# A linear-attention and gated-MLP kernel: the first batch's state add moves into a TensorE product, weight bits go through ScalarE, and the issue table is new

## The chip, the cores and the metric

The kernel runs on one core of one Trainium2 chip. The metric is device time in microseconds, from launch to end, of that one core. Three runs of the kernel before gave 377.19, 381.42 and 382.31 us.

## The reference

Four batches of 768 time steps pass through an attention with a decaying state (8 heads of 48 channels), and its output `x` (768 x 384 for each batch) through a gated layer whose gate mixes the time steps:

```python
for t in range(S):                                   # S = 768
    cur = einsum('bhd,bhe->bhde', u[None] * kt, vt)
    y[:, :, t] = einsum('bhd,bhde->bhe', rt, state + cur)
    state = wt[:, :, :, None] * state + einsum('bhd,bhe->bhde', kt, vt)
...
h = maximum(x @ w_in, 0.0)
u, v = h[..., :512], h[..., 512:]
v_n = (v - mean(v)) / sqrt(var(v) + 1e-06)
gated = u * (einsum('ts,bsd->btd', w_spatial, v_n) + b_spatial[None, :, None])
return gated @ w_out
```

Inputs and output are float32, except `w_in` and `w_out`, which are float64.

## The kernel before, in words

**Tiling.** A batch is cut into 6 chunks of 128 steps, a chunk into two halves of 64 (`x` = 0 and 1). Chunks are numbered 0 to 23 over all batches; the first batch is chunks 0 to 5. The heads are packed in pairs on 112 partitions (`R`), four pairs side by side (`G`).

**Attention of a chunk.** SyncE loads the decays `W`, the keys `kk`, the queries `rr` and the values `v` (`slot_load`). VectorE builds running products of the decays with two scans (L432 into `F`, L442 in place), then `kk*F` (L445) and `rr*W` (L447); either product may stand on GpSimd. TensorE transposes `kk*F` (L504, tile `pt`; below "the key transposes") and ScalarE copies that to `KT`; TensorE forms the state's increment `pd` for both halves (L562, 48x48 products into the PSUM tile `pp`). `slot_s` then updates the state of each half in two steps: S0 = `pd` + old state (L577 or L579, VectorE) and new state = S0 times the decay at the half's end (L582, VectorE or GpSimd). Three state tiles `SA` go round. TensorE also forms the scores (L487), which VectorE writes into `As` under a mask (L490), and sums the output in the PSUM tile `pyw` from `As` and `v` and from `rr` and the state (L516). In chunks 0 to 5 the bonus term comes from four small TensorE products (L417, tile `pg`, from `rk` = `kk`*`rr`, L412). ScalarE splits the result into a high and a low part for exact products (L600, L607), in chunks 0 to 7 with a TensorE product that subtracts the high part (L604).

**The gated layer.** Each product is three passes, high x high, high x low, low x high (`mm3`, L614 to L616): `ph` for a chunk (3 groups of three products, 512 columns), `pu`, `pv` and `po` for half batches (384 columns).

**The weights.** `split64` (L328 to L357) turns each float64 piece into a high and a low float32r part. A piece is two words per number, `dl` and `dh`; L348 scales `dh` (ScalarE or VectorE), L350 shifts that left by 3 (VectorE), L351 takes the top three bits of `dl` in (VectorE), L352 the sign. There are 10 pieces, 6 of 512 columns and 4 of 384.

**What sets the order.** All operations are collected first. The table `PLAN` names an engine and a start time for each, `plan` sorts by the start times, and the engines get their instructions in that order. Nothing on the chip waits for a time of the table: each engine takes its instructions in turn and waits only for what an instruction reads or overwrites. `fill` puts filler products (`warm`, L854, 128 x 128 of zeros into a corner of `pyw`) on TensorE where the table has a gap on it, until `last`, which stands behind chunk 5.

Of the kernel before, what the change touches and what calls it, by code (L numbers as in the profile page):

```python
# [10 lines left out]
I32 = mybir.dt.int32  # L11
AF = mybir.ActivationFunctionType
# [17 lines left out]
T19r Sdc S9l S4k6 S39x S73 Akk Vmy Vo7 Vu9 A17i G1pt Sc3 Auf Vw8 Vxh V16p A27a G29r Spa A1ek V1hp V1ka V1nn  # L30
A1po G1ut S3c S4l S5u S8c Vfg Tuv Vbj Vf0 Vh4 Vhs Aog Ghl Vl9 Axn Anx Ayb Tla Amp Tol Vq6 Grk Txe Tyf V14x
T17c T18p A1ao T1cf A1di S1f0 A1we V1zy V22k V265 A3bk G3ep Smg A162 V18e V1de V1g1 A1o0 V3lp S1xh A29v V2tt
V2v2 V2zd A36l V3p2 S3vw A4s6 V4x8 S2ic A2tg V4da S1yq A2cw G3y8 S1zz A2e2 V3u9 S450 A58r V5ch S2y9 A3fr
G40w S6e4 A6qj G7n2 S57l A5hr G5rf S6xs A7fr G7ke S218 A2gj G2lj S4vq A5bb V5gc S7wr A85w G87j S1b9 A3d0
V4el V4fo V4hb A4m1 V4o8 S2fu A2x9 V312 V324 V3jg A44m G47p S4ix A4tb V4v8 V4yj V506 A566 V57p S3l3 V3x9
V4im V4jo V4mo A532 V561 T1vz T2fn T2oz A2ro A2uw A2ye Sau Sfu Sel Skj Vz5 T11h Vr3 Vvx Vx5 V11r A159 G11a
G19k A1g0 A1a5 A1go V10u G14q T14z A18y T1at V1ch V1f3 T1gn T1ng V1pk T1s0 T1ux A1xt T1za A20e T21v T2i5
T2k2 A2q1 A2ul A2v9 Snp S10d S1a0 S1ci V1im T1kx V19b V1pc V1rd V1sm A1w3 V1lz V20v A1nq A1sb A21z V1ro G1t8
T1p5 A1r4 T1tm V1vr G1y8 T242 T253 V29i T2by T2db A2f7 T2hl A2io T2qx T2vi T2xg A332 A381 A38p A3b1 V3ch
V3c7 V3ct G3di G3ea G3i4 G3iw A3pt A3t5 V3vk A3nu A417 V45k A3lv A46t V4bm S1dr S1pe S1w8 S1tw V24h T26s  # L40
V1wr V248 V2bb V2ck A2g9 V27u G2g6 A29l A21g A2jq V2bm G2d6 T2aa A2bp T2ec V2fx V2k4 T2m9 T2na V2pf T2t4
T2uh A320 T33h A34z T385 T3e0 T3fx A3uk A40x A42m S22v S271 S2el S2h3 G2o7 T30s V2gz V2l2 V2lm V2ma A2pr
V2s5 V2wr A34p A362 G35i V2r7 V2yf T2ze A30t T34a V35v G389 T3ae T3bf V3ei T3i5 T3jh A3kt T3na A3rt T3y4
T401 T44n A4ai A4eq A4fe S2x0 S2p9 S2vr S2zi V33l T35w V36t V3aa V3d1 V3gb A3sv V3aj V3ne V3dd A3gw V3ro
V3dl V3ks T3d4 A3ej T3kj V3qs V3tc T3vd T3wf V3ye T428 T43l A45r T47g A49g T4ax T4cu T4er A4hd A4je A4k1
A4o9 V4nz V4pk G4q9 G4ss G4tk G4uc V4uz A547 A57b V594 A513 A59w V5ds V4vy A4xj V5as T572 S38o A3i0 S3mc
A3yb S419 A4c5 S4f3 A4p1 T3lu T3qr T3tn A3xa T4zs T519 T58s T5el T5hi T5iy V5ll G5or A5rn V613 T3nv T3pa
T3s7 A3w7 T5t4 T5ul T60w T64c T65t T679 V6h1 G6is A6ro V71b T480 T49h T4gp A4yz T52p T57c T5a8 T5g2 T5ro
T62c V6ja V6nq A6pd V72m T4sf T4tw T4vc A501 T545 T55l T5bp T5d5 T5ke T5lv V5nu G5u3 A5yo V6w6 T736 T74m
T763 T7bn A7dn S7f1 T71q T7a7 T7op T7q5 V7s7 S8hd T7d4 T7ek T7g0 T7hg V7pn Sac2 T4i5 T4jl T4l2 A4n6 T8jj  # L50
T8l0 T8mg T8ul T9fc T9lp V9oc G9q4 A9w2 V9xm T6dn T6f3 T6gk A6ij T7rm T7t2 T7ui T7zr T817 T8b2 V8g6 V8ht
A8jq G8qv T5nb T5os T5q8 A5t2 T7vy T7yb T86p T885 T89m T8ci V8nm V94w A9if V9n1 T4o2 T4pj T4qz A4ug T8pc
T8qt T8s9 T8w2 T91j T930 V975 G9e2 A9ux Va3r Taqj Tarz Tb0e Tb1v Ab3u Sbmd Taie Taju Tam6 Tanm Aau3 Sbjv
# [12 lines left out]
Vahy Aaqc Aaso Gaul Ab4w Ab7x Vbr7 Aalq Ab1u Gb3q S86q A8g2 S8j0 A8wp S90u A9dq S9go A9s2 T9az T9cf T9dv
# [48 lines left out]

GAP, FILL_TO = 0.8, 5

EARLY = 8

NA = 3  # L120

# [870 lines left out]
```

## Time and profile before

| what | value |
|---|---|
| three runs, median (lowest, highest) | 381.42 us (377.19, 382.31) |
| the profiled execution, its own time | 379.98 us |
| its span from the first to the last instruction | 378.2 us |
| mean granted TensorE clock | 0.963 |
| TensorE busy | 361.2 us, 95% of the span |
| VectorE, ScalarE, GpSimd busy | 253.4, 190.4, 107.0 us |

The span is 1.8 us shorter than the profiled execution's time. A granted clock of 1.00 is 2.4 GHz, 0.50 is 1.2 GHz; a stretch between holds some of both. TensorE's ends are modelled, so its busy share says that something was in its pipeline and not that the array was full. "Idle before" an instruction is time in which its engine had nothing running, and the name behind the arrow is what ended it.

### The profile page before, as it was taken

Reading aid. Unit: us, or ns where it says so; the run is one execution under the profiler, and the core shown is the slowest. Engines: PE = TensorE matmul, PEld = TensorE weight load, DVE = VectorE, ACT = ScalarE, POOL = GpSimd, SP = SyncE. Lnnn points to the kernel's source line nnn. Section 1 sums busy time; section 2 is a strip of 40 time slices with the busy share of each in tenths; the row PEclk is TensorE's granted clock in tenths of the full one; section 3 lists DMA queues with packets and bytes.
Section 4 is the critical chain, followed back from the end, with each engine's and each line's share of the span. In section 5 each row is a group of like instructions: output and inputs, shape, how many; then the busy total and the mean of one; then the engine's idle time right before and its main releaser. Section 6 shows DMA issues by size and latency. Waiting matters only on the chain.

```text
span 378.2 us, 13807 instructions
## 1 busy us (share of the span) xinstructions
PE 361.2 (95%) x5994; PEld 327.0 (86%) x5994; DVE 253.4 (67%) x491; ACT 190.4 (50%) x525; POOL 107.0 (28%) x140
## 2 busy tenths in 40 slices
PE   5799899999999999999999999999999999999995
PEld 5777678899889788999988898989989888999995
DVE  6989489999877786867577587656556754342131
ACT  2556578994456437872244138651154336722122
POOL 3505417114314242170401312144620041003111
PEclk9856599999999999999999999999999999999999
DMA  7967447673564645424233637243234420120221
GB/s 207 248 174 221 127 121 234 177 207 105 159 177 118 185 143 167 148 72 156 68 114 92 196 103 223 58 157 85 50 109 146 132 63 5 27 77 2 55 93 66
DMA packets 33023, 47.91 MB, mean 127 GB/s; under 512 B 3264, under 2 KB 21824, under 8 KB 32960
## 3 DMA queue, kind: packets, MB, share of 16 engines
q1 hardware_dynamic: 32960, 47.00, 43.0%
q8 instruction: 48, 0.79, 0.9%
q14 instruction: 15, 0.12, 0.1%
HBM read 42.27 MB, written 4.72 MB: 124 GB/s over the span
## 4 chain that ended last, share of the span: by engine, by line
PE 78%; DMA 8%; DVE 5%; ACT 4%; issue 2%; POOL 2%; SPq 1%; DVEq 0%; POOLq 0%; ACTq 0%
PE pyw L516 9%; PE pv L614 8%; PE pv L615 8%; PE pv L616 8%; PE ph L614 5%; PE ph L616 4%; PE ph L615 4%; PE pu L614 4%; PE po L614 4%; PE po L616 4%; PE po L615 4%; PE pu L615 3%; PE pu L616 3%; DMA kk<-in_tr_dram 3%; PE pp L487 3%; DMA rr<-in_tr_dram 3%
## 5 line engine op out<-in xcount | busy, mean ns | idle before, releaser
L614 PE MATMUL pv<-ws,vh 128*128 128x384 f32 x192 | 66.8, 348 | 0.0
L615 PE MATMUL pv<-ws,vh 128*128 128x384 f32 x192 | 64.9, 338 | 0.6 <-POOL ws L325 0.6
L616 PE MATMUL pv<-ws,vl 128*128 128x384 f32 x192 | 64.8, 338 | 0.0
L720 DVE TENSOR_TENSOR t<-pv,b_sb 128x384 f32<-128x384 f32 x32 | 17.7, 553 | 30.9 <-PE pv L616 30.8
L614 PEld LDWEIGHTS pv<-ws,vh 128*128 128x128 f32 x192 | 36.0, 188 | 1.3 <-ACT ws L323 0.3
L615 PEld LDWEIGHTS pv<-ws,vh 128*128 128x128 f32 x192 | 36.1, 188 | 0.9 <-POOL ws L325 0.9
L616 PEld LDWEIGHTS pv<-ws,vl 128*128 128x128 f32 x192 | 36.1, 188 | 0.0
L724 ACT CAST gh<-t 128x384 fp32r<-128x384 f32 x32 | 15.9, 512 | 38.3 <-POOL t L722 25.6
L614 PE MATMUL pu<-xT,wi 128*128 128x384 f32 x96 | 34.0, 355 | 0.0
L614 PE MATMUL po<-wo,gh 128*128 128x384 f32 x96 | 32.8, 342 | 0.0
L615 PE MATMUL pu<-xT,wi 128*128 128x384 f32 x96 | 32.4, 338 | 0.0
L432 DVE TENSOR_TENSOR_SCAN F<-W,zz 112x512 f32<-112x512 f32 x24 | 29.1, 1212 | 5.0 <-ACT zz L444 3.7
L616 PE MATMUL pu<-xT,wi 128*128 128x384 f32 x96 | 32.4, 337 | 0.0
L615 PE MATMUL po<-wo,gh 128*128 128x384 f32 x96 | 32.3, 336 | 0.0
L616 PE MATMUL po<-wo,gl 128*128 128x384 f32 x96 | 32.3, 336 | 0.0
L614 PE MATMUL ph<-wi,xT 128*128 128x512 f32 x72 | 31.5, 438 | 0.0
L582 POOL TENSOR_TENSOR SA<-S,prod 112x256 f32<-112x256 f32 x22 | 17.5, 797 | 43.9 <-DVE S L579 25.1
L616 PE MATMUL ph<-wi,xT 128*128 128x512 f32 x72 | 29.5, 409 | 0.1
L615 PE MATMUL ph<-wi,xT 128*128 128x512 f32 x72 | 29.3, 407 | 0.0
L442 DVE TENSOR_TENSOR_SCAN W<-W,zz 112x512 f32<-112x512 f32 x24 | 29.1, 1212 | 0.2
L471 ACT ACTIVATE As<-id,dg 128x64 f32<-128x64 f32 x112 | 28.3, 338 | 0.1
L600 ACT CAST xT<-pyw 128x384 fp32r<-128x384 f32 x24 | 11.5, 481 | 32.4 <-PE pyw L516 31.0
(184 smaller groups left out, 817.3 us busy)
## 6 DMA issues: line engine op xcount, KB each, us to landing
N<-in_nat_dram SPq DMA_DIRECT2D x18, 384.0 KB, 3.7
Nw<-in_gt_dram SPq DMA_DIRECT2D x16, 384.0 KB, 3.5
W<-in_tr_dram SPq DMA_DIRECT2D x24, 224.0 KB, 4.1
kk<-in_tr_dram SPq DMA_DIRECT2D x24, 224.0 KB, 3.8
rr<-in_tr_dram SPq DMA_DIRECT2D x24, 224.0 KB, 4.0
v<-in_nat_dram SPq DMA_DIRECT2D x24, 192.0 KB, 3.9
out_dram<-ot SPq DMA_DIRECT2D x24, 192.0 KB, 3.1
wst<-in_w_spT_dram SPq DMA_DIRECT2D x12, 192.0 KB, 4.5
```

Source lines behind the costliest of these rows:

```text
L432: op({"V": 1.22}, lambda: nc.vector.tensor_tensor_scan(flat(F())[:, ::-1], W[:, 2:][:, ::-1], flat(zz[:R])[:, ::-1], 0.0, ALU.mult, ALU.ma ...
L442: op({"V": 1.22}, lambda: nc.vector.tensor_tensor_scan(W[:, :n], W[:, :n], flat(zz[:R]), 0.0, ALU.mult, ALU.max), r=[("zz", 0)], w=[wk])
L471: e.mul(As()[:, h, :], id2, dg()[:, h:h + 1])
L487: nc.tensor.matmul(pa[ts, j, g, :], kk()[rs, g, ts], rr()[rs, g, ts], start=True, stop=True)
L516: nc.tensor.matmul(py[Q * n:Q * (n + 1), x, k_, :], a, b, start=(x, n) not in seen, stop=True, skip_group_check=True)
L582: op({"V": 0.42, "G": 0.617}, lambda e: e.tensor_tensor(new, S0, Wc.unsqueeze(2).broadcast_to([R, G, E2]), ALU.mult), r=[("S0",), ("Wc", i ...
L600: op({"A": 0.48}, lambda: nc.scalar.copy(part(hi), ps), r=[("py", 0)], w=[(hi, j)], banks=("PY",))
L614: nc.tensor.matmul(ps, ah, bh, start=first, stop=False)
L615: nc.tensor.matmul(ps, ah, bl, start=False, stop=False)
L616: nc.tensor.matmul(ps, al, bh, start=False, stop=last)
L720: op({"V": dve(HT)}, lambda: nc.vector.tensor_tensor(t1(), pv()[:, :HT], b_sb[:, tsl], ALU.add), r=[(pv, 0), ("b", 0)], w=[(t1, 0)])
L724: op({"A": act(HT)}, lambda: nc.scalar.copy(gh(), t1()), r=[(t1, 0)], w=[(gh, 0)])
```

## The change

Four things change.

1. **State add on TensorE** in chunks 0 to 5 (`ON_PE = 6`). `slot_pd` makes the increment of each half by itself. Behind it one product of the identity with the old state (112 rows, 256 columns, float32) adds the old state in PSUM (10 such products; the first half of chunk 0 has no old state). `slot_s` is then one step, new state = `pd` times the decay, on VectorE or as four instructions on ScalarE. Later batches keep the two steps, apart from each batch's first half, which had a copy and a product and now has the product alone.
2. **Low bits on ScalarE.** A new ScalarE instruction for each of the 10 pieces reads the top byte of `dl` and writes its top three bits as a whole number over `dl`; one VectorE instruction then shifts and combines, where two stood (L350 and L351).
3. **Filler rule.** `fill` puts in as many filler products as keep TensorE's planned share at 0.7 (`DUTY`), at most what the gap holds less 0.35 us, where before it filled each gap over 0.8 us less those 0.8 us.
4. **New table**, made with longer times for hand-overs between engines and for several TensorE steps. It moves nearly every operation.

```diff
 PLAN = """
-T19r Sdc S9l S4k6 S39x S73 Akk Vmy Vo7 Vu9 A17i G1pt Sc3 Auf Vw8 Vxh V16p A27a G29r Spa A1ek V1hp V1ka V1nn
+T5a S8c S9l S22m S5fx Sjh A15r A177 V19w V1bw A1j9 V1nu Sh0 A106 A11m V14q V187 A1ni V2f8 S1e3 A1wk A1v4
...
-GAP, FILL_TO = 0.8, 5
+GAP, FILL_TO = 0.35, 5
+
+WINDOW, DUTY = 3.41, 0.7
...
+ON_PE = 6
...
+        def low3(e, dl, dh, m):
+            by = d()[:, :2 * n].bitcast(U8).rearrange("p (n q) -> p n q", q=8)[:, :, 3]
+            e.activation(dl, by, AF.Identity, bias=third, scale=1.0 / 32)
...
-        conv({"V": one}, lambda e, dl, dh, m: V.tensor_scalar(m, m, 3, None, ALU.logical_shift_left))
-        conv({"V": two}, lambda e, dl, dh, m: V.scalar_tensor_tensor(m, dl, 29, m, ALU.logical_shift_right, ALU.bitwise_or), True)
+        op({"A": act(n)}, lambda: low3(nc.scalar, *parts()), r=[(d, 0)], w=[(d, 1)])
+        op({"V": two}, lambda: V.scalar_tensor_tensor(
+            parts()[2], parts()[2], 3, parts()[0], ALU.logical_shift_left, ALU.bitwise_or),
+           r=[(d, 1)], w=[(em, 0)], port=True)
...
+        for x in xs:
+            n = (2 * i + x) % NA
+
+            def both(x=x, old=SA[n]):
+                mm(x, False)
+                nc.tensor.matmul(pd[:R, x].rearrange("p g e -> p (g e)"), ident[:R, :R],
+                                 old.rearrange("p g e -> p (g e)"), start=False, stop=True, skip_group_check=True)
+
+            if i % NC_ or x:
+                op({"T": 0.66}, both, r=[(KT, 0), (v, 0), ("SA", n)], w=[("pd", x)], mode="squares", banks=(f"PA{x}",))
...
+        if first or i < ON_PE:
+            def decay(e):
+                if e is nc.scalar:
+                    for g in range(G):
+                        e.mul(new[:, g], pd[:R, x, g], Wc[:, g:g + 1])
+                else:
+                    e.tensor_tensor(new, pd[:R, x], Wc.unsqueeze(2).broadcast_to([R, G, E2]), ALU.mult)
...
     def fill(order):
-        t = first = 1.1
+        t, runs = 1.9, []
...
-                if t < last.start and o.start - t > GAP:
-
-                    warm((o.start - t - GAP) / (0.214 if t > first else 0.43))
-                t = max(t, o.start + o.eng["T"])
+                s, took = o.start, o.eng["T"]
+                if t < last.start:
+                    n = int(min((DUTY * WINDOW - busy(s - WINDOW, s)) / 0.214 + 0.99, (s - t - GAP) / 0.214))
+                    if n > 0:
+                        warm(n)
+                        runs.append((t, t + n * 0.214))
+                runs.append((s, s + 0.85 * took))
+                t = max(t, s + took)
```

Three places show how the table moves work. The names are the tiles of above with a running number; `zk` is the zero tile of the filler.

**SyncE, the first loads.** Before:

```order
L380 DMA W_115<-in_tr_dram 112x4x128
L384 DMA kk_145<-in_tr_dram 112x512
L384 DMA rr_147<-in_tr_dram 112x512
L333 DMA d_('wv', 0)_149<-in_w_in_dram 128x1024
L388 DMA v_151<-in_nat_dram 128x384
L888 DMA up_sb<-in_gu_dram 48x4x1
L380 DMA W_116<-in_tr_dram 112x4x128
L333 DMA d_('wv', 1)_157<-in_w_in_dram 128x1024
L888 DMA up_sb<-in_gu_dram 48x4x1
L384 DMA rr_160<-in_tr_dram 112x512
L384 DMA kk_165<-in_tr_dram 112x512
L388 DMA v_170<-in_nat_dram 128x384
```

Now:

```order
L391 DMA W_117<-in_tr_dram 112x4x128
L395 DMA rr_147<-in_tr_dram 112x512
L395 DMA kk_150<-in_tr_dram 112x512
L399 DMA v_152<-in_nat_dram 128x384
L930 DMA up_sb<-in_gu_dram 48x4x1 x2
L395 DMA rr_156<-in_tr_dram 112x512
L395 DMA kk_158<-in_tr_dram 112x512
L391 DMA W_118<-in_tr_dram 112x4x128
L338 DMA d_('wv', 1)_163<-in_w_in_dram 128x1024
L338 DMA d_('wv', 0)_166<-in_w_in_dram 128x1024
L399 DMA v_171<-in_nat_dram 128x384
```

The first two chunks' queries and keys (`rr`, `kk`) now stand ahead of the 512 KB weight pieces `d_('wv', ...)`; before, the first piece stood between chunk 0's loads and the second ahead of chunk 1's keys and queries.

**TensorE, the start.** L888 is now the filler's line, L515 the key transposes, L428 the bonus, L572 the increment, L584 the identity product, L527 the output sums, L498 the scores. Before:

```order
L854 MATMUL pyw<-zk 128x128 x13
L504 MATMUL pt_188<-ident,kk_145 128x112 x4
L562 MATMUL pp<-v_151,KT_195 48x48 x16
L854 MATMUL pyw<-zk 128x128 x5
L417 MATMUL pg_232<-up_sb,rk_163 128x2 x4
L516 MATMUL pyw<-rr_147,SA_126 32x64 x8
L487 MATMUL pp<-rr_147,kk_145 64x64 x16
L417 MATMUL pg_282<-up_sb,rk_276 128x2 x4
L504 MATMUL pt_290<-ident,kk_165 128x112 x4
L516 MATMUL pyw<-As_251,vp_121 32x64 x16
L516 MATMUL pyw<-As_251,v_151 32x64 x16
L516 MATMUL pyw<-rr_147,SA_126 32x64 x8
```

Now:

```order
L888 MATMUL pyw<-zk 128x128 x13
L515 MATMUL pt_187<-ident,kk_150 128x112 x4
L428 MATMUL pg_192<-up_sb,rk_169 128x2 x4
L888 MATMUL pyw<-zk 128x128 x3
L572 MATMUL pp<-v_152,KT_199 48x48 x8
L888 MATMUL pyw<-zk 128x128 x6
L527 MATMUL pyw<-rr_147,SA_128 32x64 x8
L498 MATMUL pp<-rr_147,kk_150 64x64 x16
L572 MATMUL pp<-v_152,KT_199 48x48 x8
L584 MATMUL pp<-SA_128,ident 112x256
L515 MATMUL pt_280<-ident,kk_158 128x112 x4
L428 MATMUL pg_288<-up_sb,rk_201 128x2 x4
```

The increment of chunk 0 is now two pieces of 8 products, the second followed by the first identity product, and the filler ahead of the scores is 3 and 6 products in place of 5. Up to the key transposes of chunk 4 there are 31 filler products, where there were 23.

**TensorE, around the key transposes of chunk 4** (`kk_615` before, `kk_604` now; `ph_2` is chunk 2's group). Before:

```order
L614 MATMUL ph_2_787<-wi_128,xT_0_0_350 128x512
L615 MATMUL ph_2_787<-wi_129,xT_0_0_350 128x512
L616 MATMUL ph_2_787<-wi_128,xT_0_1_376 128x512
L504 MATMUL pt_866<-ident,kk_615 128x112 x4
L417 MATMUL pg_873<-up_sb,rk_775 128x2 x4
L604 MATMUL pyw<-xT_1_0_881,nident 128x192 x2
L562 MATMUL pp<-v_716,KT_878 48x48 x16
L417 MATMUL pg_913<-up_sb,rk_888 128x2 x4
L614 MATMUL ph_3_923<-wi_128,xT_1_0_881 128x512
```

Now:

```order
L572 MATMUL pp<-v_519,KT_658 48x48 x8
L584 MATMUL pp<-SA_128,ident 112x256
L515 MATMUL pt_850<-ident,kk_604 128x112 x4
L648 MATMUL ph_2_759<-wi_130,xT_0_0_359 128x512
L649 MATMUL ph_2_759<-wi_131,xT_0_0_359 128x512
L650 MATMUL ph_2_759<-wi_130,xT_0_1_377 128x512
L648 MATMUL ph_2_759<-wi_130,xT_0_0_359 128x512
L649 MATMUL ph_2_759<-wi_131,xT_0_0_359 128x512
L650 MATMUL ph_2_759<-wi_130,xT_0_1_377 128x512
L638 MATMUL pyw<-xT_1_0_855,nident 128x192 x2
L428 MATMUL pg_872<-up_sb,rk_775 128x2 x4
L572 MATMUL pp<-v_684,KT_867 48x48 x8
```

Ahead of these transposes there are now 7 of the `ph` groups of three products, where there were 9, so two more of them come behind, and with them three of the ten identity products.

On VectorE the instructions from chunk 0's first scan to chunk 4's `kk*F`, which those transposes need, are 58 before and 57 now: the 7 adds, the copy and 2 decay products become 5 decay products from PSUM; 15 bit operations (three for each of 5 pieces) become 14 (1 scaling, 7 shifts with the low bits, 6 signs); 3 low-part subtractions, two more `rr*W`, one diagonal (L484) and one small copy come in; one scan and one reciprocal go out. ScalarE has 8 of the new low-bit instructions up to there. GpSimd has 5 instructions there (behind the start-up ones) where it had 13.

## Rows read from the trace of the kernel before

**Rows 1.** The page's part 2, tenths of 40 slices of 9.5 us.

```profile
PE   5799899999999999999999999999999999999995
DVE  6989489999877786867577587656556754342131
PEclk9856599999999999999999999999999999999999
```

**Rows 2.** Busy time in stretches (us busy, x instructions, granted clock).

```profile
8.40:15.90 7.50, 5.04 (x107) 4.37 (x107) 6.90 (x13) 4.13 (x14) 2.64 (x2) 1.00 1.08 258
15.90:32.90 17.00, 16.43 (x343) 13.84 (x342) 14.88 (x23) 8.88 (x26) 7.29 (x7) 0.50 0.63 169
36.40:46.60 10.20, 8.43 (x164) 6.41 (x172) 5.39 (x10) 5.53 (x19) 5.31 (x5) 0.50 0.57 166
51.98:373.80 321.82, 317.63 (x5130) 291.26 (x5128) 212.75 (x418) 162.71 (x441) 88.26 (x108) 1.00 0.40 118
```

**Rows 3.** Busy time of VectorE from its first scan to 49.2 us.

```profile
4.10:49.20 45.10, 35.67 (x58) 0.70 0.73 196
```

**Rows 4.** Who VectorE waited for from 8 to 52 us: total, times, longest.

```profile
DVE S L579 <- PE pp L562: 4.3, 2, 3.6
DVE As L490 <- PE pp L487: 3.5, 2, 2.2
DVE rk L412 <- DMA kk<-in_tr_dram: 0.3, 1, 0.3
```

**Rows 5.** Timeline of VectorE: start, us, line, operation, out<-in, idle before and its releaser.

```profile
4.10 1.22 DVE L432 TENSOR_TENSOR_SCAN F<-W,zz 112x512 f32<-112x512 f32 x1 [0.85 <-DMA W<-in_tr_dram]
6.30 0.69 DVE L412 TENSOR_TENSOR rk<-kk,rr 112x512 f32<-112x512 f32 x1 [0.78 <-DMA rr<-in_tr_dram]
17.30 2.95 DVE L352 SCALAR_TENSOR_TENSOR e_('wv', 1)_225<-d_('wv', 1)_157,e_('wv', 1)_225 128x512 int32<-128x512 int32 x1
21.95 0.67 DVE L351 SCALAR_TENSOR_TENSOR e_('wu', 1)_296<-d_('wu', 1)_193,e_('wu', 1)_296 128x512 int32<-128x512 int32 x1
...
48.61 0.68 DVE L445 TENSOR_TENSOR kk<-kk,F 112x512 f32<-112x512 f32 x1
```

**Rows 6.** Timeline of GpSimd, same columns, beside the long VectorE instruction.

```profile
17.18 1.28 POOL L447 TENSOR_TENSOR rr<-rr,W 112x512 f32<-112x512 f32 x1
18.42 1.28 POOL L355 TENSOR_TENSOR wi<-e_('wv', 0)_172,wi 128x512 fp32r<-128x512 f32 x1
```

**Rows 7.** Timeline of TensorE: filler at 10 us, the products at 51 us.

```profile
10.13 1.38 PE L854 MATMUL pyw<-zk 128*128 128x128 f32 x10
...
51.29 0.39 PE L614 MATMUL ph<-wi,xT 128*128 128x512 f32 x1
51.98 0.55 PE L504 MATMUL pt<-ident,kk 112*128 112x112 f32 x4
```

**Rows 8.** The chain that ended last: start, length, what (two loads in it).

```profile
1.79 4.42 DMA rr<-in_tr_dram
6.23 8.26 DMA kk<-in_tr_dram
```

**Rows 9.** Groups of VectorE, 4 to 60 us: busy us, mean ns.

```profile
L579 DVE TENSOR_TENSOR S<-pp,SA 112x256 f32<-112x256 f32 x9 | 3.7, 414 | 4.6 <-PE pp L562 4.6
L350 DVE TENSOR_SCALAR e_('wv', 0)_172<-e_('wv', 0)_172 128x512 int32<-128x512 int32 x1 | 0.4, 428 | 0.0
```

**Rows 10.** The same of ScalarE.

```profile
L471 ACT ACTIVATE As<-id,dg 128x64 f32<-128x64 f32 x32 | 8.1, 336 | 0.1
L348 ACT ACTIVATE e_('wv', 0)_172<-d_('wv', 0)_149 128x512 f32<-128x512 f32 x1 | 0.7, 688 | 5.9 <-DMA d_('wv', 0)_149<-in_w_in_dram 5.9
```

**Rows 11.** Who TensorE's weight loads waited for from 52 us on.

```profile
PEld pyw L516 <- DVE As L490: 2.3, 4, 1.0
PEld pv L615 <- POOL ws L325: 0.9, 1, 0.9
PEld pyw L516 <- ACT vh L684: 0.8, 1, 0.8
```

More of the change, by code (lines that the diff above doesn't have):

```diff
@@ L279 @@
     nc.gpsimd.memset(neg, -1.0)
+    third = cp.tile([P, 1], F32, name="third")
+    nc.gpsimd.memset(third, -31.0 / 64)
     nc.scalar.activation(cp.tile([P, 1], F32, name="warm"), eps, AF.Sqrt)
@@ L533, in mm @@
                         mm_y(i, x, n, SA[(2 * i + x) % NA][rs, g, half], rr()[rs, g, ts])
-        op({"T": 0.28}, mm, r=[(rr, 0)] + [("SA", (2 * i + x) % NA) for x in range(first, 2)],
+        op({"T": 0.33}, mm, r=[(rr, 0)] + [("SA", (2 * i + x) % NA) for x in range(first, 2)],
            w=[("py", 0)] + ([("fence",)] if cross else []), mode="strips", banks=("PY",))
@@ L554, in slot_pd, with mm @@
         xs = range(2 if i % NC_ < NC_ - 1 else 1)
-        def mm():
+        def mm(x, alone=True):
             for g in range(G):
-                for x in xs:
-                    for j in range(2):
-                        rows, ts = slice(64 * j, 64 * j + D), slice(L * x, L * (x + 1))
-                        h = 2 * g + j
-                        nc.tensor.matmul(pd[rows, x, g, T * j:T * j + D], KT()[ts, g, rows], v()[ts, D * h:D * (h + 1)],
-                                         start=True, stop=True)
-        op({"T": 0.375}, mm, r=[(KT, 0), (v, 0)], w=[("pd", x) for x in xs], mode="squares", banks=("PA0", "PA1"))
+                for j in range(2):
+                    rows, ts = slice(64 * j, 64 * j + D), slice(L * x, L * (x + 1))
+                    h = 2 * g + j
+                    nc.tensor.matmul(pd[rows, x, g, T * j:T * j + D], KT()[ts, g, rows], v()[ts, D * h:D * (h + 1)],
+                                     start=alone or g == 0, stop=True, skip_group_check=not alone)
+        if i >= ON_PE:
+            op({"T": 0.375}, lambda: [mm(x) for x in xs], r=[(KT, 0), (v, 0)], w=[("pd", x) for x in xs],
+               mode="squares", banks=("PA0", "PA1"))
+            return
+        for x in xs:
[7 more added lines that the diff above has]
+            else:
+                op({"T": 0.19}, lambda: mm(0), r=[(KT, 0), (v, 0)], w=[("pd", 0)], mode="squares", banks=("PA0",))
+            if x == 0:
+                slot_s(i, 0)
     def slot_s(i, x):
@@ L856, in fill, with busy @@
     def fill(order):
[L857 removed]
+        t, runs = 1.9, []
+        def busy(a, b):
+            return sum(max(0.0, min(e, b) - max(s, a)) for s, e in runs)
         for o in order:
             if o.on == "T":
[L860 to L863 removed]
+                s, took = o.start, o.eng["T"]
[6 more added lines that the diff above has]
+                t = max(t, s + took)
             yield o
```

193 lines of the change are left out of this document (97 added, 96 removed).

## The prediction, written before the change was run

> **What bounds the kernel now.** I read the page's slices first [rows 1]. TensorE is busy to the end from about 20 us on, so the run is a start-up and then a queue of TensorE work. The bottom row shows the exception: the granted clock is 1.0 throughout but for slices 2 to 5. The table of stretches [rows 2] says how much that is: from 15.9 to 32.9 us and from 36.4 to 46.6 us, 27.2 us together, TensorE ran at 0.50 (1.2 GHz) and was busy for 24.9 of them. Ahead of the first fall, from 8.4 to 15.9 us, it was busy 5.04 of 7.50 us. What it did in the slow stretches would have taken some 12 us less at 2.4 GHz.
>
> The next question is who needed TensorE there. I follow VectorE, because the state and the masked scores pass through it. From its first scan at 4.10 us to 49.20 us it ran 58 instructions, busy 35.67 of 45.10 us [rows 3], so 9.4 us were waits: 4.3 + 3.5 us for TensorE's products in `pp`, in four waits of up to 3.6 us, and 1.1 us for `rr` and `kk` from memory [rows 4, 5]. The 58th is `kk*F` of chunk 4; it ends at 49.3 us, and the key transposes of chunk 4 start at 51.98 us [rows 5, 7]. From there on the clock is full and TensorE is busy 317.6 of 321.8 us [rows 2]: the rest is work that has to be done.
>
> So the time is: when those transposes start, plus TensorE's work behind them, plus the waits in it, plus an end that the change leaves alone.
>
> **Part 1: VectorE up to the transposes.** It is not the instructions that become fewer. By the two orders 57 stand where 58 stood. From the rows: the adds and two-step updates give 10 instructions of 0.41 for 5 [rows 9], so -2.1; one scan less, -1.2 [rows 5]; two `rr*W`, three subtractions and a diagonal of the 0.68 size come in, +4.1 [rows 5]; the bit operations stay at 8.9 within 0.2 (five of 0.43 and ten of 0.68 [rows 5, 9] against one of 0.43, ten of 0.68 and three with three quarters of the columns). Together +0.8 us. The merged step saves VectorE nothing up to here, because more pieces are now done early.
>
> One instruction, the sign step at 17.30 us, took 2.95 us where its like took 0.67 [rows 5], beside two GpSimd instructions that ran from 17.18 to 19.70 us [rows 6]. Without these 2.3 us the 58 need 33.4 us, and the 57 need 34.2: from 4.1 us, when the first decays landed (they are still the first load), to 38.3 us if VectorE never waits. To that come the waits:
>
> - Memory: 1.1 us before. Chunk 1's keys were issued behind a weight piece and took 8.26 us to land [rows 8]; now they stand ahead of both. I take 0.8, the wait for `rr` [rows 5], between 0 and 1.1.
> - ScalarE: the merged step now waits for the new instruction. Eight of them come up to here, at 0.69 for 512 columns (the like is the scaling [rows 10]), 5.3 us on an engine that was busy 8.88 of 17 us and 5.53 of 10.2 us [rows 2]. It has the room; but a `KT` copy or a score diagonal can stand behind one. I take 0.5, between 0 and 1.4 (two in a row). Chunk 0's two state steps as four ScalarE instructions cost up to 4 x 0.34 us [rows 10] in place of 0.41, but VectorE has other work then.
> - GpSimd: 2.3 us of stretch before, with 13 instructions; now 5. I take 0.9 in that proportion, between 0 and 2.3.
> - TensorE: 7.8 us before, nearly all at half clock. If the clock stays up, 3.9; and since two `ph` groups of 0.69 us [rows 7] no longer stand in front, 3.0. Between 0 and 7.8.
>
> Sum 38.3 + 5.2 = 43.5 us, and 0.7 us for what stands ahead of the transposes in TensorE's queue (half an increment and an identity product): **44.2 us, 7.8 us earlier than before.**
>
> On GpSimd's share the Trainium skill has a rule, in "SBUF — State Buffer", section "Who interferes with whom": a VectorE instruction with two SBUF inputs and a GpSimd instruction that reads SBUF exclude each other, and the later one waits for the whole of the other. The one long row agrees (17.30 to 20.25 us against a GpSimd end at 19.70). By the rule at its worst this term would be larger than in proportion; that is the third rival.
>
> **Part 2: the work behind.** Two `ph` groups come behind the transposes, 2 x 0.69 = 1.4 us, and three identity products. A filler product of 128 columns takes at most 1.38/5 = 0.28 us at full clock [rows 7]; 256 columns so at most 0.55, and at least one pass's 0.12 (half the 0.23 between products of 512 columns). I take 0.45, nearer to the filler, which is float32 too. Together **2.7 us later** (1.7 to 3.0).
>
> **Part 3: the waits behind.** From 52 us on TensorE idles 4.2 us [rows 2], and its weight loads wait 4.0 us in the three largest named groups [rows 11], partly the same. The table only sets an order, so a longer hand-over delays nothing by itself; it moves a consumer behind other work. I take half of the 8.2 us as gone, **4.1 us earlier**. Nothing excludes that a new order brings waits of its own: from 8.2 earlier to 4 later.
>
> The filler is 31 products up to the transposes in place of 23. It stands in gaps; if it is late, 8 x 0.28 = 2.2 us are on the path, which the range of the TensorE wait covers.
>
> **Sum** against the profiled execution's 379.98 us: -7.8 + 2.7 - 4.1 = -9.2, so **371 us**. That execution lies 1.4 us below the median of the three runs, 381.42, which lie 5 us apart. About 2% is what a measurement of this kernel can tell from no change; from the median that is 373.8 and 389.0 us. The forecast's own range is 363 (waits behind gone, transposes at 40 us) to 376.
>
> **The rivals.**
>
> *The clock falls all the same.* For it: ahead of the fall TensorE was busy 67% of a stretch and the queue still pauses at each state step, and the bonus products hold it without much in them; the fillers are placed by the table, while VectorE drifted. Against: 8 more fillers and the first identity products lie in that stretch. If the whole slow part comes back, the TensorE wait is 7.8 again and seven identity products at twice 0.45 add 6.3 us, half of it in gaps: transposes at 52.1 us, then +2.7 - 4.1: **379**. If it is half the stretch, **375**. The Trainium skill, in "TensorE: Matmul & The Clock Gate", section "A second HAM failure mode: psum-queue depth-cycling", says that short pauses between groups of products are enough to make the clock swing. The two falls of this trace, with TensorE busy between them, agree, and it speaks against relying on the filler.
>
> *Slower: half clock and no room.* In the first slow stretch TensorE was busy 16.43 of 17.00 us [rows 2]; it was itself the limit. If the clock is low again from 16 to 46 us, identity products (6.3 us) and 8 more fillers (3.4 us at half clock) are all on the path, less the two `ph` groups moved behind (2.8 at half clock): transposes at 58.9 us; with +2.7 and nothing won behind, **390**. It decides once the low clock covers nearly all of that time and TensorE is never idle in it.
>
> *GpSimd blocks VectorE.* Each of the 5 GpSimd instructions holds a VectorE instruction for its 1.28 us [rows 6], 6.4 us in place of 0.9: **376**. For it: the stretched row. Against: it was the one of 58 that was held so long, beside 13 chances.
>
> **Chances.** Forecast 0.62, half the fall 0.12, the whole fall 0.12, GpSimd 0.08, slower 0.06. The range from 363 to 382 us leaves out the slow rival and the ends of the others, some 0.15. Under 373.8 us lie 0.9 of the forecast (0.56) and some of the 375 and 376 cases (0.08): faster 0.64. Slower 0.06, within 2% 0.30.
>
> **What would show it.** The granted clock in the stretches 15.9 to 32.9 and 36.4 to 46.6 us at 1.00 or near it: right; at 0.50: the first or second rival. VectorE's waits for `pp` up to chunk 4's `kk*F` at some 3 us and the transposes at 44 us: part 1. A VectorE instruction over 1.5 us beside a GpSimd one: the third rival. TensorE's idle time from the transposes to its last product at 2 us or less: part 3; at 4 us or more, the table has won nothing behind. I am wrong at the root if the clock stays up and the transposes still start after 50 us; then VectorE or ScalarE sets the start by itself.

## The result, and the profile after

The changed kernel took **383.72 us** (median of four runs, 382.23 to 385.14) beside 380.61 us of the kernel before: a ratio of 1.010 with a 95% interval of 1.005 to 1.015. In a later run, at the end of the experiments, it took 381.93 us beside 381.19, a ratio of 1.000 (0.995 to 1.005). So the change made the kernel slightly slower or no different, where 371 us was forecast; 383.72 lies above the forecast's range of 363 to 376. Executions more than 1.5% above a kernel's fastest are left out of ratios and intervals but not out of medians, so the two don't always divide.

The profiled execution is one of 382.99 us, with a span of 381.3 us. First the page of the changed kernel: busy tenths in 40 slices, to be laid beside [rows 1], and the queues of part 3.

```profile
PE   8897999799999999999999999999999999999995
PEclk9979699999999999999999999999999999999999
...
q8 instruction: 48, 0.79, 0.9%
```

Half of the low clock is gone: two slices under 9 stand where four stood. The table of stretches has the exact ends (columns as in [rows 2], all engines).

```profile
17.77:24.60 6.83, 6.26 (x51) 4.79 (x46) 3.83 (x9) 5.08 (x10) 1.16 (x1) 0.50 0.73 231
24.60:38.26 13.66, 11.23 (x387) 9.65 (x389) 12.17 (x20) 6.10 (x19) 1.39 (x2) 1.00 0.66 184
38.26:45.08 6.82, 6.82 (x63) 4.64 (x47) 3.76 (x7) 4.56 (x10) 1.98 (x2) 0.50 0.37 109
50.56:376.30 325.74, 321.97 (x5142) 296.69 (x5140) 216.15 (x421) 156.11 (x416) 79.23 (x99) 1.00 0.39 115
```

The clock was at 0.50 for 13.65 us in place of 27.2. Yet VectorE waited longer for TensorE than before, 8.2 us against 7.8 in [rows 4] (who VectorE waited for, 8 to 52 us):

```profile
DVE SA L609 <- PE pp L584: 5.0, 3, 3.1
DVE As L501 <- PE pp L498: 3.2, 2, 2.6
```

VectorE's timeline shows where. Its start is the one of before [rows 5].

```profile
4.10 1.22 DVE L443 TENSOR_TENSOR_SCAN F<-W,zz 112x512 f32<-112x512 f32 x1 [0.82 <-DMA W<-in_tr_dram]
...
19.83 0.42 DVE L609 TENSOR_TENSOR SA<-pp,prod 112x256 f32<-112x256 f32 x1 [1.50 <-PE pp L584]
...
25.88 0.74 DVE L501 COPY_PREDICATED As<-mask,pp 128x512 f32<-128x512 int32 x1 [2.57 <-PE pp L498]
...
34.37 1.55 DVE L366 TENSOR_TENSOR wi<-e_('wv', 1)_234,wi 128x512 fp32r<-128x512 f32 x1
...
42.27 0.43 DVE L609 TENSOR_TENSOR SA<-pp,prod 112x256 f32<-112x256 f32 x1 [3.06 <-PE pp L584]
...
48.26 0.69 DVE L456 TENSOR_TENSOR kk<-kk,F 112x512 f32<-112x512 f32 x1
```

`kk*F` of chunk 4 is 0.35 us earlier than in [rows 5], and the key transposes start at 50.56 us (TensorE's timeline), 1.4 us earlier than in [rows 7] where 7.8 were forecast:

```profile
50.04 0.69 PE L584 MATMUL pp<-SA,ident 112*112 112x256 f32 x2
50.56 0.55 PE L515 MATMUL pt<-ident,kk 112*128 112x112 f32 x4
```

Why was TensorE late? Its weight loads have two long idle times ahead of 52 us, and what ended them is "issue": no other engine, no semaphore.

```profile
15.57 0.20 PEld L527 LDWEIGHTS pyw<-rr,SA 48*32 48x32 f32 x6
17.50 0.19 PEld L527 LDWEIGHTS pyw<-rr,SA 48*32 48x32 f32 x9 [1.73 <-issue]
...
34.79 0.27 PEld L527 LDWEIGHTS pyw<-As,vp 64*32 64x32 f32 x26
37.65 0.12 PEld L527 LDWEIGHTS pyw<-As,vp 64*32 64x32 f32 x3 [2.59 <-issue]
```

Both cut a run of like products in two (6 + 9 of `rr,SA`, 26 + 3 of `As,vp`), so it isn't data that was missing. Such an idle time is called a hole below. Behind 50 us the same cause is all that TensorE's products idled for (who they waited for, 50.5 to 376.3 us):

```profile
PE pp L572 <- issue: 2.3, 1, 2.3
PE pyw L527 <- issue: 1.5, 3, 0.8
```

Numbering TensorE's records in the trace (products, weight loads and those of its sequencer together) in order of time gives the pattern: every one of these holes stands ahead of record 193 + 256 n, n a whole number. The page's part 3 has the other half: 48 transfers of 16,384 bytes on queue q8, "instruction", about one for each 256 TensorE instructions. The next table sets blocks of 256 against their fetches, worked out from the trace's TensorE records and q8 transfers. "Entered" is the first record of a block, "played" its first to last start; the fetch is the one for the block after it; the gap is from that last start to the first of the next block.

```
kernel            entered  played  fetch starts  fetch   gap behind
                     us      us    after entry   took    the block
before             33.64    4.41      3.87       1.24      2.03
changed            12.27    3.45      2.74       1.06      1.78
changed            30.71    4.30      4.52       0.99      2.64
changed            37.65    7.69      1.47       1.04      0.01
changed            45.34    3.91      0.87       1.31      0.00
changed            68.59    2.38      2.44       0.96      2.46
pad48              11.22    4.18      2.61       1.20      1.04
pad48              40.36    3.85      1.04       1.28      0.00
pad48_traffic      41.42    3.88      3.19       0.89      1.77
loads_later        32.43    4.42      2.34       1.10      0.36
pad48_wu0_later    11.65    4.03      0.60       1.27      0.00
```

In the kernel before and the changed one and all experiments there are 57 gaps over 0.3 us at such a boundary; 56 end 1.1 to 1.8 us (median 1.43) behind the end of a fetch. So a gap is the fetch's start + its 1 us + 1.4 us, less the time that the block before it played. Ahead of 70 us 157 blocks have exactly one fetch, and for 153 of them this gives the gap within 0.35 us; later some records are missing, and blocks can't be set against their fetches surely. A block of `mm3` products plays 5 us or more and hides that; a block in an attention burst (32x64 and 48x48 products, two records each) plays 2.4 to 4.5 us and doesn't, if its fetch starts late.

### The profile page after: what moved, and what is told of

Same layout as the page of the kernel before. It is cut to its first block, busy times and chain, and to the rows that moved or that the text cites. A ratio compares the mean times of both kernels' runs of the same rounds, so it can differ in the third digit from the quotient of the medians.

```text
span 381.3 us, 13822 instructions
## 1 busy us (share of the span) xinstructions
PE 366.4 (96%) x6030; PEld 333.5 (87%) x6030; DVE 256.7 (67%) x495; ACT 182.9 (48%) x486; POOL 89.5 (23%) x125
## 4 chain that ended last, share of the span: by engine, by line
PE 96%; issue 2%; DVE 1%; ACT 0%
PE pv L648 10%; PE pyw L527 10%; PE pv L650 9%; PE pv L649 9%; PE ph L648 5%; PE pu L648 5%; PE po L648 5%; PE ph L650 5%; PE ph L649 5%; PE pu L649 4%; PE pu L650 4%; PE pp L572 4%; PE po L650 4%; PE po L649 4%; PE pp L498 4%; PE pyw L888 3%
## 5 line engine op out<-in xcount | busy, mean ns | idle before, releaser
L501 DVE COPY_PREDICATED As<-mask,pp 128x512 f32<-128x512 int32 x24 | 17.8, 743 | 22.1 <-PE pp L498 12.6
L648 PE MATMUL ph<-wi,xT 128*128 128x512 f32 x72 | 31.3, 435 | 0.0
L650 PE MATMUL ph<-wi,xT 128*128 128x512 f32 x72 | 29.1, 404 | 0.0
L649 PE MATMUL ph<-wi,xT 128*128 128x512 f32 x72 | 29.0, 403 | 0.0
L677 ACT ACTIVATE hv<-ph 128x512 f32<-128x512 f32 x24 | 14.3, 596 | 30.6 <-PE ph L650 24.0
L527 PE MATMUL pyw<-rr,SA 48*32 48x64 f32 x1408 | 25.4, 225 | 3.1 <-issue 3.1
```

The lines of the kernel that those rows point to most:

```text
L501: op({"V": 0.73}, lambda: nc.vector.copy_predicated(As().rearrange("p (g j) t -> p j g t", j=2), mask.unsqueeze(1).unsqueeze(1).broadcast_ ...
L527: nc.tensor.matmul(py[Q * n:Q * (n + 1), x, k_, :], a, b, start=(x, n) not in seen, stop=True, skip_group_check=True)
L648: nc.tensor.matmul(ps, ah, bh, start=first, stop=False)
L649: nc.tensor.matmul(ps, ah, bl, start=False, stop=False)
L650: nc.tensor.matmul(ps, al, bh, start=False, stop=last)
L677: op({"A": 0.69}, lambda: nc.scalar.activation(hv(), ph(), AF.Relu, accum_out=col(0)), r=[(ph, 0)], w=[(hv, 0), (s, 0, j)])
```

## The experiments

**The theories.** F: the holes are late instruction fetches; what moves the boundaries (the changed kernel has 36 more TensorE products on record, 6030 in place of 5994) moves the holes, and they, not the steps of the change, took the gain. L: the fetch starts late because it stands behind data loads. Rivals: P, the identity products cost it; O, the new order does; W, padding helps in itself. All kernels of a group ran on one chip, beside the kernel before; times of different groups are compared by their ratios to it. A padding product is of one column, four instructions, 0.05 us; it adds zero.

**Moving the boundaries, and making the products small.** In the changed kernel, and in the kernel before:

```diff
-    op({"T": 0.1}, lambda: warm(1), w=[("pw", 0)])
+    def pad(n):
+        for _ in range(n // 4):
+            nc.tensor.matmul(pw[:1, :1], zk[:1, :1], zk[:1, :1], start=False, stop=True, skip_group_check=True)
+
+    op({"T": 0.1}, lambda: (pad(48), warm(1)), w=[("pw", 0)])
```

(160 in place of 48 in *pad160*, 40 in the kernel before), and, alone, the ten identity products of `slot_pd` (256 columns each by the trace; the 288 of the expectation is wrong):

```diff
-                nc.tensor.matmul(pd[:R, x].rearrange("p g e -> p (g e)"), ident[:R, :R],
-                                 old.rearrange("p g e -> p (g e)"), start=False, stop=True, skip_group_check=True)
+                nc.tensor.matmul(pd[:1, x, 0, :1], ident[:1, :1],
+                                 old[:1, 0, :1], start=False, stop=True, skip_group_check=True)
```

> The changed kernel with 12 products of one column (48 more TensorE instructions) ahead of the first filler, so that every 256th instruction falls 48 places earlier in the work. Theory F (fetch): TensorE's holes in the trace after the change stand at every 256th instruction because the next 256 are not fetched yet; the two at 15.7 and 35.0 us move to other work, all holes over 0.3 us sum to 3 to 5 us instead of 7.8, chunk 4's key transposes start at 46 to 49 us instead of 50.6, and the time is 376 to 380 us. Theory P (the identity products are the cost) and theory O (the new order is): the holes stay where they are in the work, transposes at 50 to 51, time 382 to 384.

> The same with 40 such products (160 instructions). Theory F: by the records' own pace the least holes of all shifts, one of about 0.8 us ahead of 52 us, 3 to 5 us in all; transposes at 45 to 48 us, time 375 to 379. Theories P and O: 382 to 385, the padding costing under 1 us.

> The kernel before with 10 such products (40 instructions) ahead of its first filler. Theory F: the boundaries of 256 fall into faster stretches (by the pace of the records 9 us of holes against 3.6 where they are now), so this kernel becomes slower by 3 to 6 us: 383 to 387. Theories P and O: no change, 380 to 381.5.

> The changed kernel with each of the ten identity products (288 columns) replaced by one of a single column, so the number and places of the instructions stay; the old state is then not added in the first batch. Theory F: the holes at 15.7 and 35.0 us stay at the same instructions, time 379 to 382.5. Theory P: the products are what delays the first batch, transposes 4 us or more earlier than 50.6 and time 372 to 377. Theory O: 381 to 383.

*pad48*: 376.11 us, ratio to before 0.988 (0.979 to 0.997), where the changed kernel had 1.010 and 1.000: twelve tiny products are worth 1 to 2%. One hole of 1 us is left ahead of 52 us, at 15.4 us, and one clock fall, 17.09 to 27.33 us; the transposes start at 45.77 us. Theory O had the holes stay where they were; with the same order they moved and the time fell, so the order by itself isn't what made the loss. VectorE's waits from 8 to 52 us are 4.5 us:

```profile
DVE As L501 <- PE pp L498: 3.2, 1, 3.2
DVE SA L609 <- PE pp L584: 1.3, 2, 0.6
```

*pad160*: 378.38 us, 0.996 (0.993 to 1.000), below the changed kernel's 1.010 but not to be told from its later 1.000, and not the best shift that the pace of the records had promised. Its profiled execution took 383.18 us, 4.8 us above the median, and is left out but for the count of gaps above.

*Before, padded by 40*: 380.18 us, 0.998 (0.993 to 1.003). The expectation of 3 to 6 us slower missed. Two things were wrong in it. In that table the first filler operation stands behind chunk 1's transposes (17.87 us), and the padding ran at 20.3 us, so earlier boundaries stayed; and the pace alone doesn't make a hole: of 11 blocks that played under 5 us, fetches in 8 started soon enough, and the gaps over 0.3 us sum to 1.9 us, less than the 3.9 of the unpadded trace.

*Small products*: 381.43 us, 0.998 (0.993 to 1.003), with the same two holes at the same instructions:

```profile
17.98 0.28 PEld L527 LDWEIGHTS pyw<-rr,SA 48*32 48x32 f32 x9 [2.40 <-issue]
...
37.88 0.12 PEld L527 LDWEIGHTS pyw<-As,vp 64*32 64x32 f32 x3 [2.65 <-issue]
```

So P falls: without the products' columns the transposes start at 49.94 us, the time hardly moves (0.998 beside 1.000 and 1.010), and the holes stay. The clock was low for 17.1 us in this trace, 13.65 in the changed kernel's, so a small cost of the products may be hidden; the four microseconds and more of theory P are not there.

**The control, and the loads.** *pad256* has 71 padding products and seven of the first fillers fewer, 256 instructions more in all. *loads_later* moves three loads of the changed kernel behind chunk 4's `kk` in the table, *pad48_wu0_later* two of pad48 behind chunk 2's; *pad48_traffic* adds a copy of 1 MB within DRAM to pad48.

```diff
 pad256:            pad(284) as above, and in fill
-                        warm(n)
+                        warm(n - 7 if len(runs) == 1 else n)
 loads_later:       wu 1 26.41 -> 30.00, u 26.86 -> 30.05, wst 3 27.31 -> 30.10   (kk 4: 29.94)
 pad48_wu0_later:   wu 0 11.37 -> 14.45, wo 1 11.82 -> 14.50                      (kk 2: 14.39)
 pad48_traffic:     ahead of the load of wst 2
+                nc.sync.dma_start(dp.tile([P, 4 * FH], I32, name="idle"), w_in[:P, :].bitcast(I32))
```

> The changed kernel with 71 products of one column ahead of its first fillers and seven fillers fewer there (28 instructions): 256 TensorE instructions more, so every boundary of 256 falls where it fell without padding, and the first transposes start when they did. Theory F: the holes return at the same work as in the changed kernel (ahead of chunk 3's and behind chunk 1's products, 1.5 to 3 us each), transposes of chunk 4 at 49 to 52 us, time 381 to 385. If it was padding as such that helped (theory W: small products ahead of the fillers change the clock or the start): 375 to 379.

> The changed kernel with three loads (0.9 MB: wu 1, u, wst 3) issued behind chunk 4's kk instead of ahead of it. Theory L (the fetch at 35.2 us starts 4.5 us after TensorE enters the block, because it stands behind loads of 28 to 33 us): it starts 1 to 2.5 us after the entry, the hole of 2.4 us at 35.0 falls under 0.8, the one at 15.7 stays, transposes at 47.5 to 49.5, time 378 to 382. If loads have no part in it: the fetch 4 us or more after entry, hole over 2 us, time 382 to 385.

> The kernel with 48 padding instructions, and 1 MB copied within DRAM (data that nothing reads) issued at 37 us, ahead of the load of wst 2. Theory L: the fetch in the block entered at 40.4 us, which played 3.85 us and had no hole, starts 2 us or more later than the 1.04 us after entry that it had; a hole of 1.5 to 4 us follows near 44 us; time up by 1 to 4 us against the 376.1 of the kernel without the copy. If fetches don't stand behind loads: fetch at 1 to 1.5 us, no hole, time within 1 us.

> The kernel with 48 padding instructions, and two loads of weights (0.9 MB: wu 0, wo 1) issued behind chunk 2's kk instead of ahead of it. Theory L: the fetch in the block entered at 11.2 us starts 1 to 1.5 us after the entry instead of 2.6, the hole of 1.0 us at 15.4 is gone, the one clock fall that was left is shorter or gone, transposes at 43 to 45.5, time 372 to 376. Against it: the same hole, or wu 0 late for ScalarE (its first use is planned 5 us behind the new place), 376 to 378.

*pad256*: 381.17 us, 1.005 (1.001 to 1.009). The first hole is back at the very instruction where the changed kernel has it, between the 6th and the 9 last of `rr,SA`:

```profile
18.69 0.21 PEld L527 LDWEIGHTS pyw<-rr,SA 48*32 48x32 f32 x9 [2.21 <-issue]
```

The second did not come in the profiled execution (its fetch started 2.0 us after entry, not 4.5), and the transposes start at 49.08 us. Against pad48 there are 236 more padding instructions and 28 fewer of the filler; by the ratios it is some 6 us slower, of which the padding itself is at most 3.0 us (it took 3.6 us, against 0.6) and takes the place of fillers. More padding doesn't help: theory W falls.

*loads_later*: 380.76 us, 1.003 (0.999 to 1.007). The hole at 35 us, now at 36.9, shrank as expected, the fetch 2.34 us after entry:

```profile
37.21 0.12 PEld L527 LDWEIGHTS pyw<-As,vp 64*32 64x32 f32 x3 [0.31 <-issue]
```

This alone does not show L: in pad256 and in the changed kernel run again (below), with these loads where they were, the same hole was missing or 0.62 us long, its fetch 2.0 and 2.73 us after entry. The hole at 15.7 us stayed (2.19 us); transposes at 47.83 us. In the changed kernel the loads issued between 28 and 33.5 us, ahead of the fetch at 35.2, are these three and five more, some 2.3 MB by the page's sizes (two rows of SyncE's timeline):

```profile
28.41 1.43 SPq L338 DMA_DIRECT2D d_('wu', 2)_514<-in_w_in_dram  x1
...
30.42 0.38 SPq L338 DMA_DIRECT2D d_('wu', 1)_523<-in_w_in_dram  x1
```

*pad48_traffic*: 378.48 us, 0.989 (0.984 to 0.994); the fetch after the copy came 3.19 us after entry and made a hole where pad48 has none, and a clock fall at 49.17 us behind it:

```profile
47.07 0.11 PEld L532 LDWEIGHTS pyw<-As,v 64*32 64x32 f32 x3 [1.72 <-issue]
```

The trace agrees with L: in six traces of kernels with 48 or 40 padding instructions and no copy the fetch of this block started 0.4 to 1.0 us after entry. The expected 1 to 4 us of time are not shown, since the ratios, 0.989 and 0.988, are the same.

*pad48_wu0_later*: **374.59 us, 0.983 (0.978 to 0.989)**, the lowest median of those that compute everything. The hole at 15.4 us is gone. Here L rests on many traces: the fetch of this block started 2.6 to 3.7 us after entry (at 13.8 to 16.0 us) in the seven traces with the two loads ahead of it, and 0.2 to 1.0 us after (at 12.1 to 12.9 us) in this one and four of those below that keep them later; in the fifth, small_fillers, it started at 12.65 us too, in a block entered 2 us earlier. A new hole of 1.82 us came at 25.3 us, its fetch 3.03 us after entry, with a clock fall of 3.4 us behind it. Transposes at 44.79 us. Who TensorE waited for behind them:

```profile
PE pyw L527 <- issue: 1.4, 2, 0.7
```

**What the parts of the change are worth once the holes are out of the way**, from that kernel ("base"): the third load later and 40 instead of 48; the small products; small fillers (the 18 behind the first 13 as products of one column); the low bits on VectorE.

```diff
 pad40_three_loads: pad(40), and wo 0 18.93 -> 22.25 (kk 3: 22.17)
 small_fillers:
-                        warm(n)
+                        (warm if len(runs) == 1 else lambda m: pad(4 * m))(n)
 low_bits_vectore:  ten table entries from ScalarE to VectorE, right ahead of the merge, and
-        op({"A": act(n)}, lambda: low3(nc.scalar, *parts()), r=[(d, 0)], w=[(d, 1)])
+        conv({"V": one}, lambda e, dl, dh, m: V.tensor_scalar(m, m, 3, None, ALU.logical_shift_left))
         (the merge as in the kernel before)
```

> The kernel with padding and two loads of weights behind chunk 2's kk (374.6 us), with 40 padding instructions instead of 48 and a third load (wo 0, 0.4 MB) issued behind chunk 3's kk instead of ahead of it: the fetch that was 3.0 us late at 24.6 us. Theories F and L: no hole over 0.5 us ahead of 52 us, no clock fall there, transposes at 42.5 to 44.5 us, time 371.5 to 374.5. Against: a hole at another place ahead of 52 us, 374 to 377.

> The same kernel of 374.6 us (48 padding instructions, two loads later) with each of the ten identity products replaced by one of a single column; the old state is then not added in the first batch. What the products cost once fetches are out of the way: by the prediction's price of 0.45 us each, of which two or three lie on VectorE's path, 0.5 to 2 us: 372.5 to 374. Theory P: 4 us or more, 368 to 371.

> The same kernel of 374.6 us with the 18 fillers behind the first 13 replaced by products of one column (the same number of instructions). If fillers keep the clock up where no fetch stalls (the prediction's step): at least one more clock fall of 7 us or more ahead of 35 us, time 377 to 381. If the clock falls come from fetch holes alone: no other fall than the one at 28 us, 373.5 to 376.

> The same kernel of 374.6 us with the low bits of the ten weights extracted by VectorE again (a shift of 0.42 us and the old merge, by the code before) right ahead of where VectorE merges them, ScalarE's ten conversions gone. By the prediction's price VectorE's path to chunk 4's transposes is 6 x 0.42 us longer, less what lies beside waits for TensorE: transposes 1.5 to 3 us later than 44.8, time 376 to 378. If VectorE's path doesn't set the end: 374 to 375.

*pad40_three_loads*: 376.38 us, 0.989 (0.985 to 0.994). No fetch hole ahead of 52 us, as forecast; but `wu 0` was now late, ScalarE and VectorE stood for it, and TensorE for ScalarE, with a clock fall from 21.63 us behind that (TensorE's timeline):

```profile
21.02 1.33 PE L888 MATMUL pyw<-zk 128*128 128x128 f32 x7 [3.19 <-ACT xT L641]
```

So here a clock fall followed a pause of TensorE that was no fetch hole; a fetch is one cause of a pause among others.

*Small products*: 374.05 us, 0.980 (0.975 to 0.985), not to be told from the base. The clock was low for 10.2 us from 18.51 us, against 3.4 us in the base, behind a pause that was no fetch hole (TensorE's timeline), so the ten products may cost more than the difference of 0.5 us:

```profile
19.31 2.08 PE L888 MATMUL pyw<-zk 128*128 128x128 f32 x8 [1.48 <-ACT xT L641]
```

*Small fillers*: 379.76 us, 0.999 (0.996 to 1.003): 5 us slower than the base, at a mean granted clock of 0.957 to 0.966 in ten of its twelve runs (0.948 and 0.953 in the two longest) against 0.995 to 1.000 in three of the base's four (0.977 in the longest). The fillers earn their place. *Low bits on VectorE*: 375.52 us, 0.987 (0.983 to 0.991), within the base's interval. In its profiled execution the clock never fell ahead of 370 us, and the one wait of VectorE from 8 to 52 us that the view lists is this:

```profile
DVE rk L421 <- PE pg L426: 0.3, 1, 0.3
```

with transposes at 45.50 us, 0.7 later than the base. The expected 1.5 to 3 us did not come: VectorE's waits for TensorE fell from 3.8 us in the base to 0.3, so the extra instructions filled time in which it otherwise waits.

**The holes behind 52 us, and the changed kernel again.**

```diff
-            prog.last = last = op({"T": 0.1}, lambda: warm(1), r=[(vn[0, c][0], 0)], w=[("pw", 0)])
+            prog.last = last = op({"T": 0.1}, lambda: (pad(96), warm(1)), r=[(vn[0, c][0], 0)], w=[("pw", 0)])
```

> The kernel of 374.6 us (48 padding instructions at the start, two loads later) with 96 more padding instructions at the last filler, at 113 us. Theory F: the two holes behind 52 us (0.9 us each at 140.6 and 171.3) go, by the records' pace one of 0.3 to 0.5 us stays near 255; less 1.2 us for the padding itself: time 373.5 to 374.8, TensorE's work behind the transposes of chunk 4 from 323.0 to 322.5 us. Without theory F: both holes stay, 375 to 376.

> The changed kernel once more, beside the aligned one on the same chip. Theory F: holes over 1 us at 15.7 us and at 35 us as before, two clock falls, 380 to 384 us, 6 to 9 us above the aligned kernel. If the first profile was a chance of one execution: holes elsewhere or none, 376 to 380.

*pad_late*: 377.21 us, 0.990 (0.984 to 0.996): not faster, and by its interval not surely slower than the base. The two late holes went, and one of 0.4 us idle came at 260 us, all as theory F says; but from the transposes to the last product it took 325.4 us in place of 323.0. Set beside the base product by product, TensorE lost 1.5 us up to the end of the padding (1.2 of it the padding itself), gained 0.9 us twice where the holes had been, and lost 1.0 us to a wait for ScalarE at 145 us, 0.7 to the new hole and 0.9 in smaller steps. The expectation of the time missed.

*changed_again*: 381.93 us. The first hole recurs at the same instruction, and longer; the second was short this time, 0.62 us, and one clock fall came, of 13.7 us from 18.36 us, where two were expected; transposes at 49.2 us:

```profile
18.55 0.28 PEld L527 LDWEIGHTS pyw<-rr,SA 48*32 48x32 f32 x9 [2.84 <-issue]
...
39.27 0.12 PEld L527 LDWEIGHTS pyw<-As,vp 64*32 64x32 f32 x3 [0.62 <-issue]
```

The place of a hole is fixed by the program; its length varies between executions (1.73 and 2.84 us for the first, 2.59 and 0.62 for the second), and why was not tried.

## Why the prediction was wrong

| step | forecast | changed | pad48_wu0_later |
|---|---|---|---|
| low clock ahead of 52 us | none | 13.65 us | 3.4 us |
| VectorE waits for TensorE, 8 to 52 us | 3.0 us | 8.2 us | 3.8 us |
| key transposes of chunk 4 | 44.2 us | 50.56 us | 44.79 us |
| TensorE busy behind them, against 317.6 before | +2.7 us | +4.3 us | +4.0 us |
| TensorE idle behind them, against 4.2 before | -4.1 us | -0.4 us | -2.8 us |

**The step that failed** is the TensorE term of part 1: "7.8 us before, nearly all at half clock. If the clock stays up, 3.9 [...], 3.0." It scaled a wait with the clock and took every wait for `pp` for work in TensorE's queue. The term measured 8.2 us. The condition failed, with 13.65 us of low clock, and a part of TensorE's lateness was neither work nor clock as the sum had them: the fetch holes, 1.73 and 2.59 us directly, and the two clock falls that begin 2.1 and 3.3 us after the holes do. That the holes bring the falls is not tried by itself, but in pad48, pad256, loads_later and the changed kernel run again, where the second hole is gone or under 0.7 us, the second fall is gone too, and in pad48_wu0_later the first hole and its fall are. With the boundaries elsewhere and two loads later the term measured 3.8 us and the transposes came 0.6 us from the forecast. Of the 12.2 us between the sum's 370.8 and the profiled 382.99 us, 6.4 lie ahead of the transposes, 1.6 in the work and 3.7 in the waits behind them, 0.6 at the end. The forecast could have seen it: the trace of before has such a hole, 1.87 us at 38 us, in the second slow stretch of [rows 2], and I read it as part of the low clock (timeline of its weight loads):

```profile
37.72 0.49 PEld L516 LDWEIGHTS pyw<-As,v 64*32 64x32 f32 x18
40.08 0.20 PEld L516 LDWEIGHTS pyw<-As,v 64*32 64x32 f32 x11 [1.87 <-issue]
```

That added products move all later boundaries was in none of the rivals.

The Trainium skill, in "Runtime: NRT & Kernel Launch", section "Instruction fetch mechanics", describes the blocks of 256 instructions and calls the cost of crossing a boundary "mostly hidden". The trace agrees for 40 of the changed kernel's 46 boundaries behind 12 us (no gap over 0.3 us) and not for six, which cost some 8 us.

**Other steps of part 1.** VectorE's instructions were priced within 0.8 us: 35.92 us busy up to `kk*F` against 34.2 and 0.9 for GpSimd. The long instructions beside GpSimd came twice, 1.55 us at 34.37 us and 1.26 at 42.61, 1.4 us in all; the third rival's 6.4 us did not. Memory cost VectorE one wait of 0.39 us behind the first scan, where 0.8 were taken. From the end of `kk*F` (48.95 us) to the transposes it was 1.6 us, not 0.7: a run of output sums from 48.45 us stood in TensorE's queue ahead of the increment and the identity product.

**Part 2** was 1.3 to 1.6 us short: TensorE's busy time behind the transposes rose by 4.0 to 4.3 us, not 2.7, for the 12 records that were expected there (six of `ph`, six of the identity). A pair of identity passes takes 0.52 us to the next product (50.04 to 50.56 us), 0.45 were taken, which is 0.2 us of it; the rest is open.

**Part 3** was right that the old waits would go. Behind 52 us TensorE's products waited seven times for another engine before, 3.5 us together (and 0.6 us of "issue"); in the changed kernel no such wait is left. But their place was taken by 3.8 us of fetch holes (2.3 and 1.5 us in the list above), which in pad48_wu0_later are 1.4. The 4.1 us taken was half of 8.2, a sum that held the idle time of the products (4.2) and that of the weight loads, partly the same; of the 4.2 alone it was nearly all.

**The rivals.** The first (the clock falls all the same, for half the stretch) had its sign: half the low clock came back. But its 375 us did not follow, since the holes' own time and what VectorE lost to them was not in it. The slower rival wanted the low clock for nearly all of 16 to 46 us; it was low for 13.65. What I said would prove the sum wrong at its root was transposes behind 50 us with the clock up; they came behind 50 us with the clock low for half the time of before, and the cause I named with it, VectorE or ScalarE by itself, was not it.

**What is left open.** The fastest version lies 3.6 us above the forecast: 0.6 from the transposes, 2.5 from work and waits behind them, 0.6 from the end of the run (4.9 us from the last product to the last instruction, 4.3 before). That the two late holes are not simply to be had back, pad_late shows. What the new order is worth by itself no run shows. Why the fetch needs 1.4 us from its end to the next instruction was not tried, nor by which path loads delay it.

## What to carry to other kernels

Idle time of TensorE that ends in "issue" inside a run of like products is worth numbering: if it stands at a multiple of 256 of the instruction stream, it is the program's length ahead of it that put it there, and a few tiny products where TensorE is idle anyway move it. Before a change that adds or removes small TensorE products is judged, compare it at two or three alignments; here 48 padding instructions alone took the ratio from 1.010 or 1.000 to 0.988, while neither the identity products nor the low bits could be told from no change. Keep large loads from being issued just ahead of a dense burst of small products, and sum the gain of a faster engine only after asking what else it waits for.

## What the hardware showed unasked

- A fetch of 16,384 bytes, about 256 TensorE instructions, took 0.9 to 1.6 us in 744 of 770 cases (2.3 at most), and a block that waited for it started 1.4 us after its end. In the changed kernel, beside 2.3 MB of loads, a fetch started 4.5 us after TensorE entered the block.
- Twelve fetch holes of 1 us and more ahead of 52 us, over nine traces of the changed kernel and its variants (pad160's left out), were each followed by a fall of the granted clock from 1.00 to 0.50, 1.7 to 3.9 us after the hole began. Holes of 1.0 to 2.5 us behind 52 us were followed by none. Both falls of the kernel before, at 15.88 and 36.36 us, had no fetch hole of 0.5 us or more ahead of them.
- The clock came back in 3.4 to 13.7 us in all of these cases. Before the change it stayed low for 17.1 us in the first fall and 10.2 in the second.
- Products of 1 x 1 went through TensorE at 0.0125 us an instruction, 48 of them in 0.6 us.
